# An attention stage's list scheduler with another model of transfers, and six load buffers instead of nine

## The chip, the cores and the metric

The kernel runs on one core of one Trainium2 chip. The metric is the device time of one execution, in microseconds. The kernel before takes 1522.84 us (median of 3 runs, 1522.7 to 1524.69).

## The reference

Three layers in float32, each fed by the one before. Attention has 8 batches, 8 heads, 576 query rows and head size 64; K and V are averaged over groups of 8 rows first, so that each query row sees 72 keys. Its output is read as 4608 tokens of 512 numbers for a mixture of 8 experts, in which each expert takes 576 tokens by a greedy choice over all logits; a gated layer follows.

```python
k_p = k.reshape(B, H, Sp, 8, D).mean(axis=3)
v_p = v.reshape(B, H, Sp, 8, D).mean(axis=3)
scores = np.matmul(q, k_p.transpose(0, 1, 3, 2)) / np.sqrt(D)
attn = np.exp(scores - scores.max(-1, keepdims=True))
attn = attn / (attn.sum(-1, keepdims=True) + 1e-9)
x = np.matmul(attn, v_p)                  # -> tokens, (4608, 512)
logits = x @ w_gate                       # expert e of each token, capacity 576
out[mask_e] = np.maximum(x[mask_e] @ w1[e], 0) @ w2[e]
y = (1 / (1 + np.exp(-(x2 @ wg))) * (x2 @ wv)) @ wo
```

## The kernel before

The program has three parts, one after another: `attention`, `experts` with the `Router` (which chooses the tokens), and `Gated`. The change touches `attention` and its scheduler alone.

Attention works on 18 tiles of 256 query rows: two for each batch (rows 0 to 511) and, after batches 3 and 7, one mixed tile with the last 64 rows of four batches. K and V come in 12 pieces each (`plan_kv`, L335): a load of 768 KB by SP's queue, three halvings that add pairs of rows (L341; VectorE for the first five K pieces, GpSimd for the others), a transpose on TensorE (L351) and a copy by ScalarE into kpT or vT (L357). From vT and the gate's weights (padded) TensorE makes the values of a batch, already multiplied by the gate (`plan_wv`, L382), which ScalarE copies into one of two buffers `wv` (L369). Three transfers inside the chip, the shift (L390 to L392, issued by ScalarE for batches 0 to 2 and by SP for the others), lay the same values out a second time at other partitions; a fourth (L394) copies them into `vmix` for the mixed tile. A buffer of wv may be written again, two batches later, when its tiles are done and its shift and vmix copy have landed.

For each tile, q is loaded by SP (L318; L323 with four small transfers for a mixed tile; two buffers of two tiles each), transposed (L411) and copied (L369). Chunks of two or three heads then go through scores (L448, `sps`), row maximum and subtraction on VectorE (L464, L468), exponential on ScalarE (L471), transposes (L484) and copies (L492), the product with the values (L509, L504, L518, `aps`), and VectorE's scaling by the row sums into `xt` (L526 to L533) and of the logits (L539, L542). SP stores the finished xt into `x_rows` (L551, L555). xt has three buffers, so a tile's first write waits for the store three tiles earlier.

The order of all engines' work is set by `Plan`, a list scheduler that runs while the program is built. Each operation has a cost on one or more engines; at each step `run` collects the operations that could start (`best`), takes those that start within 0.25 of the earliest, and emits the one of lowest rank (`go`). `go` also sets when the results are there. In the kernel before, a transfer of `size` > 0 runs on one path at 350 KB per us after those before it, and one of `size` < 0 (shift, vmix copy, stores of xt) ends a fixed time after its issue and takes nothing from the path:

```python
if x.size > 0:
    self.dma = max(self.dma, x.end + 1.3) + x.size / 350e3
    x.end = self.dma + 0.7
elif x.size < 0:
    x.end += 2.5 - x.size / 100e3
```

The plan's numbers only set the order; on the chip every engine waits for semaphores. Each transfer of SP and ScalarE takes the next of eight semaphores in rotation, and its issue waits until the transfer that held it has landed, with everything behind it in the same queue. The number of buffers of each tile stands in `BUFS`; `kv=9` are the loaded pieces of K and V.

Behind attention come the router's keys (`key_steps`; parts of it are scheduled in VectorE's gaps, L844 to L875), the first search over them, and then the experts.

Of the kernel before, what the change touches and what calls it, by code (L numbers as in the profile page):

```python
# [69 lines left out]
class Flow:  # L70
# [11 lines left out]
    def op(self, lanes, f, after=(), reads=(), makes=None, rank=0):  # L82
        x = Op(lanes, f, [a for a in after if a is not None], list(reads), makes, rank)
        if "tensor" not in lanes:
            self.todo.append(x)
        return x
# [68 lines left out]
class Plan(Flow):  # L155


    def __init__(self, nc):
        super().__init__(nc)
        self.dma = 0.0  # L160
        self.between = lambda gap: None
        self.held = {"vector": deque(maxlen=16), "gpsimd": deque(maxlen=16)}

    def op(self, lanes, f, after=(), reads=(), makes=None, rank=0, size=0, alone=False):
        x = Op(lanes, f, [a for a in after if a is not None], list(reads), makes, rank)
        x.size, x.alone = size, alone
        for b in x.reads:
            b.left = (b.left or 0) + 1
        self.todo.append(x)
        return x  # L170
# [16 lines left out]
    def best(self, x):  # L187
        at = self.ready(x)
        if at is None:
            return None  # L190
        lane = min(x.lanes, key=lambda n: max(self.t[n], at) + x.lanes[n])
        start = max(self.t[lane], at)
        if x.alone:
            for a, z in self.held["gpsimd" if lane == "vector" else "vector"]:
                if a <= start < z:
                    start = z
        return start, lane
# [13 lines left out]
    def go(self, x, lane, start):  # L211
        if lane == "tensor":
            self.between(start - self.t[lane])
        if x.makes is not None and x.makes.ap is None:
            self.free[x.makes.tag].popleft()
        x.f(getattr(self.nc, lane))
        x.lane, x.start = lane, start
        x.end = self.t[lane] = start + x.lanes[lane]
        if x.alone:
            self.held[lane].append((start, x.end))  # L220
        if x.size > 0:
            self.dma = max(self.dma, x.end + 1.3) + x.size / 350e3
            x.end = self.dma + 0.7
        elif x.size < 0:
            x.end += 2.5 - x.size / 100e3
        for b in x.reads:
            b.left -= 1
            b.end = max(b.end, x.end)
            if b.left == 0:
                self.free[b.tag].append(b.end)  # L230
        self.todo.remove(x)


def attention(tc, c, q, k, v, w_gate, xD, L, router, scr):
    nc = tc.nc
    ident = c["ident"]
    with ExitStack() as ctx:
# [21 lines left out]

        fl = Plan(nc)  # L260
        fl.t["gpsimd"], fl.t["vector"], fl.t["sync"] = 6.0, 3.0, 1.0
        BUFS = dict(kv=9, q2=2, qps=4, sps=1, aps=2, mx=3, sd=3, e=7, eT=4, qT=5, rs=3, xt=3)
        for tag, n in BUFS.items():
            fl.give(tag, n)
        count = {"av": 0}
# [26 lines left out]
        of_mix = {n: [y for y, (ti, _, _) in enumerate(chunks) if tiles[ti][1] is None and tiles[ti][0] == n] for n in range(2)}  # L292
# [8 lines left out]
        R = {}  # L301
# [9 lines left out]
        def load_q(ti, halves, rank):  # L311
            n, b, jj = tiles[ti]
            t = Buf("q2", None)
            for h0, h1 in halves:
                def f(eng, h0=h0, h1=h1):
                    qt = tile_of(t, loads, [128, H, 4, D])
                    if b is not None:
                        eng.dma_start(qt[:, h0:h1].rearrange("p h r d -> p h (r d)"),  # L318
                                      dram(q, b * H * S * D + h0 * S * D, [[4 * D, 128], [S * D, h1 - h0], [1, 4 * D]]))
                        return  # L320
                    for s in range(2):
                        for r in range(2):
                            eng.dma_start(qt[64 * s:64 * s + 64, :, r, :],  # L323
                                          dram(q, (4 * n + 2 * s + r) * H * S * D + 512 * D, [[D, 64], [S * D, H], [1, D]]))
                R["lq", ti, h0] = fl.op({"sync": 0.6 if b is not None else 2.4}, f, makes=t, rank=rank, size=(h1 - h0) * 131072)
            return t

        def plan_kv(ch, name, rank):
# [44 lines left out]
        def plan_wv(b, rank):  # L373
            free = [R["av", y] for y in of_b.get(b - 2, [])] + ([R["shift", b - 2], R["shiftm", b - 2]] if b > 1 else [R["wv1"]] * b)
            done = []
# [12 lines left out]
            def shift(eng):  # L388
# [1 line left out]
                eng.dma_start(w[72:108, 1], w[0:36, 0])  # L390
                eng.dma_start(w[0:36, 2], w[36:72, 0])
                eng.dma_start(w[36:108, 3], w[0:72, 0])  # L392
            R["shift", b] = fl.op({"scalar": 2.4} if b < 3 else {"sync": 2.2}, shift, after=done + free, rank=rank, size=-350000 if b < 3 else -165000)
            R["shiftm", b] = fl.op({"sync": 0.6}, lambda eng: eng.dma_start(vmix[:, b % 4], wv[b % 2][0:72, 0]),  # L394
                                   after=done + [R["av", y] for y in (of_mix[0] if b > 3 else [])], rank=rank + 5, size=-165000)

        def plan_q(ti):
            n, b, jj = tiles[ti]
# [55 lines left out]
        def plan_chunk(y, out):  # L454
            ti, h0, nh = chunks[y]
# [92 lines left out]
            def store(eng):  # L548
# [4 lines left out]
                for s in range(2):  # L553
                    for r in range(2):
                        eng.dma_start(dram(xD, ((4 * n + 2 * s + r) * S + 512) * DM, [[DM, 64], [1, DM]]),  # L555
                                      xt[64 * s:64 * s + 64, r].rearrange("p h d -> p (h d)"))
            fl.op({"sync": 0.6 if b is not None else 2.4}, store, after=[n2], reads=[out], rank=y, size=-524288)

        def loads_of(b):
            r = fb[b] - 12  # L560
# [1269 lines left out]
```

## Time and profile before

| | |
|---|---|
| median of 3 runs | 1522.84 us (1522.7 to 1524.69) |
| the profiled execution | 1523.92 us, span 1522.3 us |
| TensorE busy | 1467.1 us, 96% |
| weight loads busy | 1314.7 us, 86% |
| VectorE busy | 1059.7 us, 70% |
| ScalarE busy | 538.3 us, 35% |
| GpSimd busy | 395.7 us, 26% |
| moved by DMA | 294.22 MB, mean 193 GB/s |

Busy time is a sum over the whole span. Attention is the first 175 us or so, and there the engines are much less even than the sums say. In the section below, PE is TensorE, PEld its weight loads, DVE VectorE, ACT ScalarE, POOL GpSimd and SP the engine that issues most transfers; SPq is its queue. A wait is named by who waited and by what came last. Names like `kv` are the program's buffers, with their numbers left out.

### The profile page before, as it was taken

Reading aid. Unit: us, or ns where it says so; the run is one execution under the profiler, and the core shown is the slowest. Engines: PE = TensorE matmul, PEld = TensorE weight load, DVE = VectorE, ACT = ScalarE, POOL = GpSimd, SP = SyncE. Lnnn points to the kernel's source line nnn. Section 1 sums busy time; section 2 is a strip of 40 time slices with the busy share of each in tenths; the row PEclk is TensorE's granted clock in tenths of the full one; section 3 lists DMA queues with packets and bytes.
Section 4 is the critical chain, followed back from the end, with each engine's and each line's share of the span. In section 5 each row is a group of like instructions: output and inputs, shape, how many; then the busy total and the mean of one; then the engine's idle time right before and its main releaser. Section 6 shows DMA issues by size and latency. Waiting matters only on the chain.

```text
span 1522.3 us, 27187 instructions
## 1 busy us (share of the span) xinstructions
PE 1467.1 (96%) x10625; PEld 1314.7 (86%) x10625; DVE 1059.7 (70%) x2344; ACT 538.3 (35%) x1063; POOL 395.7 (26%) x416
## 2 busy tenths in 40 slices
PE   7889799999999999998999999999999999999997
PEld 5789669999999999997788888888888889999996
DVE  6688788889889977327778845666555764674564
ACT  4566232443434444334434322222321322232221
POOL 6870041353334422244323220012100120011001
PEclk9999789999999999999999999999999999999999
DMA  9974245356545686137655574535445365656651
GB/s 336 304 250 161 98 143 205 95 179 225 190 130 176 206 262 197 62 128 280 239 218 205 186 267 141 221 139 202 185 173 200 111 257 214 235 191 239 249 193 43
DMA packets 109330, 294.22 MB, mean 193 GB/s; under 512 B 12589, under 2 KB 43345, under 8 KB 94993
## 3 DMA queue, kind: packets, MB, share of 16 engines
q1 hardware_dynamic: 101636, 270.48, 50.0%
q0 software_dynamic: 6496, 20.98, 4.1%
q8 instruction: 84, 1.38, 0.4%
q10 hardware_dynamic: 1068, 1.03, 0.3%
q14 instruction: 46, 0.37, 0.1%
HBM read 222.33 MB, written 66.08 MB: 189 GB/s over the span
## 4 chain that ended last, share of the span: by engine, by line
PE 81%; DVE 8%; DMA 5%; issue 2%; ACT 1%; POOL 1%; SPq 0%; POOLq 0%; DVEq 0%; ACTq 0%
PE pj L1667 18%; PE hps L607 12%; PE acc L607 12%; PE Yg L1569 7%; PE Yv L1569 7%; PE Xg L1569 5%; PE Xv L1569 4%; PE Zg L1569 4%; PE Zv L1569 4%; PE rps L607 2%; PE aps L509 2%; DVE cx L607 1%; PE qps L484 1%; PE sps L448 1%; DMA q<-in_q_dram 1%
## 5 line engine op out<-in xcount | busy, mean ns | idle before, releaser
L607 PE MATMUL acc<-hh,w 128*128 128x288 f32 x1024 | 245.7, 304 | 0.0
L607 PE MATMUL hps<-xh,w 128*128 128x288 f32 x1024 | 235.3, 300 | 1.8 <-DVE hl L607 1.7
L1681 DVE TENSOR_TENSOR stg<-pj,stg 128x512 f32<-128x512 f32 x180 | 123.8, 689 | 109.0 <-PE pj L1667 108.1
L607 PEld LDWEIGHTS hps<-xh,w 128*128 128x128 f32 x1024 | 174.7, 189 | 3.0 <-DVE hl L607 2.4
L607 PEld LDWEIGHTS acc<-hh,w 128*128 128x128 f32 x1024 | 176.7, 189 | 0.2
L607 PE MATMUL acc<-hl,w 128*128 128x288 f32 x512 | 151.5, 296 | 0.9 <-DVE hl L607 0.9
L607 PE MATMUL hps<-xl,w 128*128 128x288 f32 x512 | 151.5, 296 | 0.1
L607 POOL TENSOR_TENSOR w<-stg,w 128x512 fp32r<-128x512 f32 (+1 forms) x81 | 119.5, 1489 | 116.2 <-ACT w L607 110.1
L607 ACT ACTIVATE hh<-hps 128x288 fp32r<-128x288 f32 x128 | 52.6, 411 | 252.4 <-PE hps L607 237.2
L1569 PE MATMUL Yg<-w 128*128 128x512 f32 (+1 forms) x540 | 126.9, 370 | 3.8 <-ACT w L1467 3.8
L1569 PE MATMUL Yv<-w 128*128 128x512 f32 (+1 forms) x540 | 126.2, 369 | 0.0
L1569 PEld LDWEIGHTS Yg<-w 128*128 128x128 f32 x540 | 99.9, 189 | 20.0 <-ACT w L1467 4.1
L607 POOL DMA_INDIRECT xg<-x_rows,idxs x48 | 46.4, 968 | 250.3 <-DVE capv L607 93.2
L1569 PEld LDWEIGHTS Yv<-w 128*128 128x128 f32 x540 | 99.4, 189 | 13.1 <-DVE vc L1605 0.4
L1667 PE MATMUL pj<-woh,xg 128*128 128x512 f32 x396 | 98.8, 391 | 1.5 <-DVE woh L1536 0.7
L1667 PE MATMUL pj<-woh,cw 128*128 128x512 f32 x396 | 98.7, 390 | 0.0
L607 PEld LDWEIGHTS acc<-hl,w 128*128 128x128 f32 x512 | 97.0, 189 | 1.1 <-DVE hl L607 1.1
L607 PEld LDWEIGHTS hps<-xl,w 128*128 128x128 f32 x512 | 96.8, 189 | 0.3 <-DVE xl L607 0.3
L1635 ACT ACTIVATE sg<-sg 128x512 f32<-128x512 f32 (+1 forms) x90 | 53.0, 589 | 122.6 <-DVE sg L1606 73.4
L607 DVE SCALAR_TENSOR_TENSOR hl<-hps,hh 128x288 fp32r<-128x288 f32 x128 | 57.4, 452 | 54.6 <-ACT hh L607 53.4
L607 ACT ACTIVATE w<-stg 128x512 fp32r<-128x512 f32 (+1 forms) x138 | 81.0, 638 | 35.8 <-DMA stg<-in_moe_w_dram 30.5
L1667 PEld LDWEIGHTS pj<-woh,xg 128*128 128x128 f32 x396 | 73.9, 188 | 17.3 <-DVE woh L1536 1.1
(280 smaller groups left out, 2968.4 us busy)
## 6 DMA issues: line engine op xcount, KB each, us to landing
w<-w_split SPq DMA_DIRECT2D x84, 1024.0 KB
stg<-in_moe_w_dram SPq DMA_DIRECT2D x30, 1024.0 KB
w_split<-w SPq DMA_DIRECT2D x21, 1024.0 KB
woh<-wo_split SPq DMA_DIRECT2D x24, 512.0 KB
wr<-wo_split SPq DMA_DIRECT2D x12, 1024.0 KB
kv<-in_k_dram SPq DMA_DIRECT2D x12, 768.0 KB
kv<-in_v_dram SPq DMA_DIRECT2D x12, 768.0 KB
x_cols<-x SPq DMA_DIRECT2D x16, 576.0 KB
```

The costliest lines, as they stand in the source:

```text
L448: eng.matmul(p[cs, r, G * j:G * j + G], t.ap[rs, h % 4, cs], kpT[rs, b if b is not None else 4 * n + 2 * c + r, h], start=True, stop=True)
L484: eng.transpose(p[:z, j], flat[:, a:a + z], ident)
L509: eng.matmul(p[:, a + s:a + s + 2], t[:, j + s], flat[:, x0:x1 + 1:x1 - x0], start=a + s == 0, stop=True, skip_group_check=True)
L607: r = f(*args, **kw)
L1569: eng.matmul(t, W(a, k), X(b, k), start=first and n == 0, stop=n == 5, skip_group_check=True)
L1635: x = fl.op(A, lambda eng: eng.activation(T(g), T(g), AF.Sigmoid), after=[op], rank=rank)
L1667: eng.matmul(self.tile(ps), G(a), W(b), start=n == 0, stop=n == 5)
L1681: y = fl.op({"vector": 0.69}, lambda eng: eng.tensor_tensor(A(), self.tile(ps), A(), op=OP.add), after=[x, st["acc", u, i]], reads=[ps], r ...
```

## The change

`Plan` now keeps the landing times of all transfers (`flights`). A transfer can start no earlier than the eighth before it has landed. A transfer from SP runs on the one path whatever its kind, at a rate of its own: 350 KB per us, and 110 for shifts and vmix copies. An operation that issues several transfers counts as so many (`dmas`), each with its share. ScalarE's shifts take places among the eight, not the path. `kv` has six buffers.

```diff
+        self.flights = [0.0] * 8
...
-    def op(self, lanes, f, after=(), reads=(), makes=None, rank=0, size=0, alone=False):
+    def op(self, lanes, f, after=(), reads=(), makes=None, rank=0, size=0, alone=False, rate=350e3, dmas=1):
         x = Op(lanes, f, [a for a in after if a is not None], list(reads), makes, rank)
-        x.size, x.alone = size, alone
+        x.size, x.alone, x.rate, x.dmas = size, alone, rate, dmas
...
         start = max(self.t[lane], at)
+        if x.size:
+            start = max(start, self.flights[-8] + 0.1)
...
-        if x.size > 0:
-            self.dma = max(self.dma, x.end + 1.3) + x.size / 350e3
+        if x.size and lane == "sync":
+            for i in range(x.dmas):
+                x.end = max(x.end, self.flights[-8] + 0.4)
+                self.t[lane] = x.end
+                self.dma = max(self.dma, x.end + 1.3) + x.size / x.dmas / x.rate
+                self.flights.append(self.dma + 0.7)
             x.end = self.dma + 0.7
-        elif x.size < 0:
-            x.end += 2.5 - x.size / 100e3
+        elif x.size:
+            x.end += 2.5 + 2 * x.size / x.rate
+            self.flights += [x.end] * x.dmas
...
-        BUFS = dict(kv=9, q2=2, qps=4, sps=1, aps=2, mx=3, sd=3, e=7, eT=4, qT=5, rs=3, xt=3)
+        BUFS = dict(kv=6, q2=2, qps=4, sps=1, aps=2, mx=3, sd=3, e=7, eT=4, qT=5, rs=3, xt=3)
...
-                R["lq", ti, h0] = fl.op({"sync": 0.6 if b is not None else 2.4}, f, makes=t, rank=rank, size=(h1 - h0) * 131072)
+                R["lq", ti, h0] = fl.op({"sync": 0.6 if b is not None else 2.4}, f, makes=t, rank=rank, size=(h1 - h0) * 131072, dmas=1 if b is not None else 4)
...
-            R["shift", b] = fl.op({"scalar": 2.4} if b < 3 else {"sync": 2.2}, shift, after=done + free, rank=rank, size=-350000 if b < 3 else -165000)
+            R["shift", b] = fl.op({"scalar": 2.4} if b < 3 else {"sync": 2.2}, shift, after=done + free, rank=rank, size=336384, rate=110e3, dmas=3)
             R["shiftm", b] = fl.op({"sync": 0.6}, lambda eng: eng.dma_start(vmix[:, b % 4], wv[b % 2][0:72, 0]),
-                                   after=done + [R["av", y] for y in (of_mix[0] if b > 3 else [])], rank=rank + 5, size=-165000)
+                                   after=done + [R["av", y] for y in (of_mix[0] if b > 3 else [])], rank=rank + 5, size=168192, rate=110e3)
...
-            fl.op({"sync": 0.6 if b is not None else 2.4}, store, after=[n2], reads=[out], rank=y, size=-524288)
+            fl.op({"sync": 0.6 if b is not None else 2.4}, store, after=[n2], reads=[out], rank=y, size=524288, dmas=1 if b is not None else 4)
```

The lines of the changed kernel stand eight further down from `go` on (L318 is L326 there, L394 is L402, L551 is L559). No instruction of attention is added or removed; they change places, up to the last of attention, and the order behind it is the same on every engine.

SP's queue, from the eighth load of K and V on (first before, then now). `q_232` and `q_255` are q of batch 2; the vmix copy from `wv_124` is batch 0's.

```order
L335 DMA kv<-in_k_dram 128x3x512 x2
L335 DMA kv<-in_v_dram 128x3x512 x2
L335 DMA kv<-in_k_dram 128x3x512
L318 DMA q_232<-in_q_dram 128x4x256 x2
L335 DMA kv<-in_v_dram 128x3x512
L335 DMA kv<-in_k_dram 128x3x512 x2
L394 DMA vmix<-wv_124 72x584
```

```order
L343 DMA kv<-in_k_dram 128x3x512 x2
L326 DMA q_255<-in_q_dram 128x4x256 x2
L343 DMA kv<-in_v_dram 128x3x512 x2
L343 DMA kv<-in_k_dram 128x3x512
L402 DMA vmix<-wv_124 72x584
L559 DMA x_rows<-xt 128x1024
```

The vmix copy moved ahead of one V and two K loads, and q of batch 2 ahead of two V loads and a K load.

SP's queue around the first mixed tile's q (`q_816` before, `q_774` now), before and now:

```order
L551 DMA x_rows<-xt 128x1024
L394 DMA vmix<-wv_124 72x584
L335 DMA kv<-in_k_dram 128x3x512
L335 DMA kv<-in_v_dram 128x3x512
L323 DMA q_816<-in_q_dram 64x8x64 x4
L551 DMA x_rows<-xt 128x1024 x2
```

```order
L326 DMA q_594<-in_q_dram 128x4x256 x2
L343 DMA kv<-in_v_dram 128x3x512
L559 DMA x_rows<-xt 128x1024
L331 DMA q_774<-in_q_dram 64x8x64 x4
L402 DMA vmix<-wv_124 72x584
L559 DMA x_rows<-xt 128x1024
L343 DMA kv<-in_k_dram 128x3x512 x2
L343 DMA kv<-in_v_dram 128x3x512
L559 DMA x_rows<-xt 128x1024
```

The K and V loads that stood ahead of the four transfers now stand behind them and behind the next store.

VectorE at the end of attention, before and now; `L<-lm` is the last reduction of the logits, and kh, u, C, EoU and kl belong to the router's keys.

```order
L533 TENSOR_TENSOR xt<-aps,rs 128x2x128
L539 TENSOR_TENSOR lm<-aps,rs 128x2x16
L542 TENSOR_REDUCE L<-lm 128x16
L864 TENSOR_TENSOR T_105<-M,U 128x10
L866 CAST kh<-V 128x10
L868 TENSOR_SCALAR u<-u 128x10
L870 TENSOR_TENSOR C<-kh,tr_77 128x10x15
L873 SCALAR_TENSOR_TENSOR EoU<-P,T_105 128x80
L875 CAST kl<-u 128x10
```

```order
L878 TENSOR_TENSOR C<-kh,tr_77 128x10x15
L881 SCALAR_TENSOR_TENSOR EoU<-P,T_105 128x80
L883 CAST kl<-u 128x10
L534 TENSOR_SCALAR rs<-aps 128x4
L535 RECIPROCAL rs<-rs 128x4
L541 TENSOR_TENSOR xt<-aps,rs 128x2x128
L547 TENSOR_TENSOR lm<-aps,rs 128x2x16
L550 TENSOR_REDUCE L<-lm 128x16
```

The six operations on these columns moved ahead of the last tile's scaling.

## Rows read from the trace of the kernel before

**Rows 1.** The page's head: the span of the profiled execution.

```profile
span 1522.3 us, 27187 instructions
```

**Rows 2.** Busy time by stretch; columns in its first line (PEclk: granted share of 2.4 GHz).

```profile
core 0: us, PE busy (x) PEld busy (x) DVE busy (x) ACT busy (x) POOL busy (x), PEclk, DMA share, GB/s
...
44.00:50.00 6.00, 0.69 (x4) 0.70 (x4) 0.86 (x2) 1.15 (x3) 5.69 (x7) 0.69 0.98 303
50.00:54.00 4.00, 4.00 (x21) 3.91 (x20) 0.89 (x4) 1.54 (x5) 3.11 (x3) 0.61 1.02 364
54.00:76.00 22.00, 21.65 (x367) 20.39 (x365) 16.91 (x55) 14.50 (x34) 19.96 (x18) 1.00 1.06 289
76.00:82.00 6.00, 3.22 (x35) 2.56 (x38) 3.40 (x9) 3.35 (x9) 5.29 (x26) 0.87 0.87 297
82.00:88.00 6.00, 6.00 (x61) 5.86 (x55) 3.64 (x12) 3.31 (x8) 5.08 (x19) 0.56 0.97 346
...
100.00:152.00 52.00, 50.03 (x817) 45.73 (x816) 45.13 (x153) 33.85 (x78) 9.47 (x12) 1.00 0.49 154
```

**Rows 3.** Waits of TensorE in the attention stage, 0 to 176 us.

```profile
PE qps L351 <- DVE kv L341: 6.4, 2, 3.8
PE qps L411 <- ACT wv L369: 5.6, 1, 5.6
PE sps L448 <- DVE sd L468: 2.5, 2, 1.4
...
PE aps L509 <- DVE lm L539: 1.3, 1, 1.3
```

**Rows 4.** Waits of all engines, 0 to 260 us: two that ended with a transfer.

```profile
ACT wv L369 <- DMA vmix<-wv: 6.6, 1, 6.6
...
DVE xt L533 <- DMA x_rows<-xt: 5.9, 2, 5.0
```

**Rows 5.** Timeline of SP's queue: start us, us until the last was issued, what.

```profile
16.58 4.14 SPq L335 DMA_DIRECT2D kv<-in_v_dram  x2
...
25.87 2.35 SPq L318 DMA_DIRECT2D q<-in_q_dram  x2
...
33.99 2.44 SPq L335 DMA_DIRECT2D kv<-in_k_dram  x2
37.55 0.95 SPq L394 DMA_DIRECT2D vmix<-wv  x1
...
58.20 0.34 SPq L551 DMA_DIRECT2D x_rows<-xt  x1
...
62.21 8.36 SPq L323 DMA_DIRECT2D q<-in_q_dram  x4
70.68 3.77 SPq L551 DMA_DIRECT2D x_rows<-xt  x2
```

**Rows 6.** Timeline of all engines, 0 to 60 us: a transpose that frees a buffer.

```profile
20.95 0.55 PE L351 MATMUL qps<-identf,kv 128*128 128x128 f32 x3
```

**Rows 7.** Timeline of all engines, 38 to 70 us: the first stall's end.

```profile
48.85 0.41 ACT L369 ACTIVATE wv<-qps 72x288 f32<-72x288 f32 x1 [6.65 <-DMA vmix<-wv]
...
49.31 1.11 PE L411 MATMUL qps<-identf,q 128*128 128x128 f32 x4 [5.57 <-ACT wv L369]
```

**Rows 8.** Timeline of all engines, 70 to 105 us: the second stall's end.

```profile
78.32 0.56 DVE L533 TENSOR_TENSOR xt<-aps,rs 128x384 f32<-128x384 f32 x1 [5.04 <-DMA x_rows<-xt]
```

**Rows 9.** Groups of instructions by shape, 0 to 178 us: GpSimd's three halvings.

```profile
L341 POOL TENSOR_TENSOR kv<-kv 128x768 f32<-128x768 f32 x19 | 34.6, 1823 | 15.5 <-DMA kv<-in_v_dram 15.4
...
L341 POOL TENSOR_TENSOR kv<-kv 128x384 f32<-128x384 f32 x19 | 19.7, 1038 | 1.3
...
L341 POOL TENSOR_TENSOR kv<-kv 128x192 f32<-128x192 f32 x19 | 11.3, 592 | 1.5
```

**Rows 10.** Timeline of VectorE: router's key work after the last reduction of the logits.

```profile
174.96 0.16 DVE L864 TENSOR_TENSOR T<-M,U 128x10 f32<-128x10 f32 x1
...
175.62 0.17 DVE L875 CAST kl<-u 128x10 f32<-128x10 int32 x1
```

## The prediction

> **What bounds the kernel now.** I looked at the span first, then at busy time by stretch, then at TensorE's waits in the stage that the change touches, and last at SP's queue in that stage, because the change only reorders attention. The profiled execution took 1523.92 us, 1522.3 of them span [rows 1], so 1.6 lie around it. It stands 1.1 us above the median of the three runs shown (1522.84) and inside their range.
>
> In most of the program TensorE is the bound, and after attention every engine's order is the same in both kernels. So an attention stage that ends earlier moves the rest forward by as much, and only its waits matter. In [rows 2] the reader is to see how uneven the stage is: from 100 to 152 us TensorE is busy 50.03 of 52 us at full clock; from 44 to 50 us it does 0.69 of 6; from 76 to 82 us 3.22 of 6. After both holes the granted clock is low: 0.61 of full from 50 to 54 us and 0.56 from 82 to 88 us, where 0.5 is the lower level of 1.2 GHz. What the engine did before each fall is nearly nothing for five microseconds in the first, two waits close together in the second. The DMA share is 0.98 in the first hole and 0.87 in the second, with hardly less around them, while from 100 to 152 us it is 0.49: everything is loaded early, and small urgent transfers share the path with loads that nobody needs yet.
>
> TensorE's own waits [rows 3] name four: 6.4 us for halved rows (3.8 at the start, so 2.6 later), 5.6 for ScalarE's copy into wv, 1.4 at most for sd, 1.3 for lm. Behind two of these stands a transfer [rows 4]: ScalarE waited 6.6 us for the vmix copy, VectorE 5.0 us for a store of xt.
>
> **First hole: the vmix copy.** Batch 2's rows may enter wv only when batch 0's copy from wv to vmix has landed. SP issued that copy at 37.55 us, after the two K loads of 33.99 us [rows 5]; ScalarE went on at 48.85 and TensorE at 49.31, after 5.57 us of nothing [rows 7]. From the issue's end (38.50) to the release are 10.3 us, which the copy spent behind other loads. The first pair of lists shows the change: two K loads and one V load fewer stand ahead of it. At the 303 GB/s of the first hole [rows 2] these 2.36 MB are 7.8 us, 2.2 more than the hole is long. q of batch 2 moves ahead of two V loads; its two parts (1.05 MB, 3.5 us at that rate) delay V. That V was issued from 16.58 us on [rows 5] and feeds the copies into wv that wait in the hole, more than 20 us later; halving a piece takes GpSimd 1.82 + 1.04 + 0.59 = 3.45 us [rows 9]. Between load and use there is room for both, so I cost the delay at nothing; if this cover is gone it is at most 3.5 us. I take the hole as removed: 5.6 us. The clock comes with it: 4.00 us of work at 0.61 lost 4.00 x 0.39 = 1.6 us, and the 0.69 us before it at half clock lost 0.3. **First term: 5.6 + 1.9 = 7.5 us.**
>
> **Second hole: the store of xt.** xt has three buffers, so a tile's first write waits for the store of the tile three before. The store of 70.68 us stood behind four transfers of the mixed tile's q, which took SP from 62.21 to 70.57 because each waited for a place among eight [rows 5], and those places were held by K and V loads. VectorE then stood 5.04 us [rows 8], TensorE 1.3 and 1.4 [rows 3], and 6.00 us at 0.56 lost 6.00 x 0.44 = 2.6. The second pair of lists: the four still come before a store, but the K and V loads that stood right ahead of them now follow that store, and the places that the four need were last held by parts of q, a vmix copy and a store. **Second term: 1.3 + 1.4 + 2.6 = 5.3 us.**
>
> **Tail.** Six operations of the router's keys ran after the last reduction of the logits, from 174.96 to the last one's start at 175.62 [rows 10]; now they stand ahead of it (third pair), in slots where VectorE waits for the last tiles. **Third term: 0.7 us.**
>
> **Six buffers instead of nine.** A load now waits for the transpose six loads earlier. The fifth and sixth waits of this kind decide: V of batch 2's second piece waits for a transpose that ended at 21.50 us [rows 6], where SP issued it at 20.72 [rows 5]. That is 0.8 us later, with other loads in flight and the DMA share near 1, so it costs nothing on the path; if it did, 0.8 us. The wait for halved rows of 2.6 us stays: the same K pieces are loaded and halved in the same order.
>
> **The remaining moves** are TensorE's and VectorE's order over 18 tiles. K and V of batches 4 to 7 are now halved, transposed and copied between those tiles' work and not before it. No row shows the cost. Below, nothing or a gain: the holes already counted hold all the waits of more than 2.6 us that are named. Above, one more wait like the first hole with its clock, 7.5 us. Nearer than either is how full TensorE is in an undisturbed stretch: 0.35 us idle in 22 where loads are plenty, 1.97 in 52 later [rows 2]. If the 50 us after the first hole run like the latter, that is 1.9 - 0.8 = 1.1 us more; a shift of wv (three issues, then a landing that no row isolates) that comes a little late twice would add about 2. I take 3 us.
>
> **Sum.** 7.5 + 5.3 + 0.7 - 3 = 10.5 us. From 1523.9 that is 1513.4; from the median it would be 1512.3. I forecast 1513.
>
> **A rule that speaks against it.** In the first hole the buffers are full and TensorE still waits, so depth is not what it lacks. The Trainium skill (Perfetto Trace Analysis, "Optimization Strategy") says that gaps that recur on the engine that should be saturated can mean too few buffers for the next tile. By that rule three buffers fewer would open gaps; the trace agrees with it nowhere in this stage, since no wait of TensorE ends with a K or V buffer coming free. The third rival works out what it would do.
>
> **The rivals.**
> *Only one hole closes.* The vmix copy also needs one of eight places, and the one it takes is held by a shift that ScalarE issues into the same crowded path; if that lands late, the copy still lands after 44 us. Then the second term and the tail remain: 5.3 + 0.7 - 3 = 3 us, 1521; or the first alone: 7.5 + 0.7 - 3 = 5.2, 1519. For it: landing took 10 us in this queue. Against it: three loads fewer. Chance 0.17, about half of it within 0.2% of before.
> *The model does not match the chip.* The planner's new rates (350 GB/s, 110 GB/s for copies inside the chip) set an order that the chip runs otherwise, and the waits come at other places for the same sum: 1520 to 1526. For it: 256-byte pieces of the mixed tile's q, which one rate cannot describe; the DMA moved 289 GB/s there with its share at 1.06 [rows 2]. Against it: the urgent copies really come earlier in SP's list. Chance 0.10.
> *Loads come too late (slower).* With six buffers and the loads of batches 4 to 7 behind stores that wait for VectorE, a piece reaches the path: 0.79 MB at 303 GB/s is 2.6 us, halving 3.45, together 6.0, and each such hole lowers the clock as above, 1.9 more. One or two eat part or all of the gain; from three (23.7 us against 13.5) the kernel is slower, 1534. For it: the stores from 70.68 us held the queue for 3.77 us [rows 5]. Against it: those loads stand tens of rows of SP's list ahead of their use, and the path is half idle after 100 us. Chance 0.08.
>
> **How the numbers follow.** 0.2% is 3.0 us, about what a measurement of this kernel tells from no change. The forecast has 0.65 (1507 to 1518: all terms and no new wait give 1523.9 - 13.5 = 1510.4 against the profiled run, 1509.3 against the median, and 2.6 more if the wait for halved rows goes too; on the other side 7.5 for new waits gives 1517.9). Faster by over 3.0 us: 0.65 + 0.08 = 0.73 and 0.02 of the second rival, 0.75. Within: 0.09 + 0.06 = 0.15. Slower: 0.02 + 0.08 = 0.10. For 8 in 10 the range goes from 1507 up to 1521, into the first rival.
>
> **What would show it.** Right: no wait of ScalarE for vmix and none of VectorE for x_rows above 1 us; the granted clock full from 30 us to the last tile; the last reduction of the logits near 164 us instead of 174.7; the six key operations before it; the router's phase and all after it as long as before. Wrong in the first step: ScalarE's copy into wv still waits for vmix between 40 and 50 us. Wrong in the costs at nothing: TensorE's transposes of kv wait for GpSimd, or aps for a shift of wv, after 50 us. The forecast falls if attention ends within 3 us of where it ended.

## The result and the profile of the changed kernel

The changed kernel takes **1507.12 us** (median of 4 runs, 1506.83 to 1510.05), the kernel before 1522.77 beside it (4 runs, 1522.06 to 1524.69): ratio 0.9900, 95% interval 0.9882 to 0.9917. That is 15.65 us less, where the forecast was 1513 in a range from 1507 to 1521: the sign was right, the gain too small by a third, and the time lies just above the lower end of that range. The profiled execution took 1506.83 us, its span 1505.2.

The same view as [rows 2], of the changed kernel:

```profile
core 0: us, PE busy (x) PEld busy (x) DVE busy (x) ACT busy (x) POOL busy (x), PEclk, DMA share, GB/s
...
44.00:50.00 6.00, 5.69 (x90) 5.15 (x87) 4.00 (x13) 2.30 (x6) 1.39 (x3) 1.00 1.11 299
50.00:54.00 4.00, 3.06 (x24) 2.82 (x24) 2.87 (x11) 2.45 (x7) 3.07 (x3) 1.00 0.91 230
54.00:76.00 22.00, 21.27 (x354) 19.68 (x353) 18.88 (x60) 14.78 (x33) 14.73 (x14) 1.00 1.02 334
76.00:82.00 6.00, 6.00 (x101) 5.77 (x95) 5.51 (x18) 3.64 (x9) 5.65 (x15) 1.00 1.05 392
82.00:88.00 6.00, 6.00 (x78) 5.46 (x77) 5.39 (x22) 5.09 (x14) 5.66 (x12) 1.00 1.05 372
...
100.00:152.00 52.00, 48.72 (x764) 45.03 (x765) 46.77 (x155) 30.94 (x72) 20.38 (x47) 1.00 0.51 167
```

From 44 to 50 us TensorE is now busy 5.69 us of 6 where it was 0.69, from 76 to 82 us 6.00 where it was 3.22, and the granted clock is 1.00 in every one of these stretches. From 50 to 54 us it idles for 0.94 us of 4, which it did not before, and from 100 to 152 us it does less (48.72 us of 52 against 50.03). Its waits up to 176 us, as in [rows 3]:

```profile
PE qps L359 <- DVE kv L349: 3.8, 1, 3.8
...
PE qps L359 <- POOL kv L349: 1.9, 3, 0.9
...
PE sps L456 <- DVE sd L476: 1.5, 3, 0.8
...
PE aps L517 <- ACT eT L500: 1.4, 2, 0.9
```

The wait for ScalarE's copy into wv (5.6 us) is gone, and so is the second wait for rows halved by VectorE: 6.4 us in two became 3.8 in one, the one at the start. In its place stand three short waits for GpSimd's halving, 1.9 us together. No wait of ScalarE for vmix and none of VectorE for x_rows is left in attention, which answers [rows 4]. SP's queue, as in [rows 5]:

```profile
31.52 0.94 SPq L402 DMA_DIRECT2D vmix<-wv  x1
...
36.95 3.59 SPq L326 DMA_DIRECT2D q<-in_q_dram  x2
...
42.67 4.59 SPq L331 DMA_DIRECT2D q<-in_q_dram  x4
...
51.59 0.45 SPq L559 DMA_DIRECT2D x_rows<-xt  x1
```

The vmix copy is issued at 31.52 us instead of 37.55. The four transfers of the mixed tile's q are issued from 42.67 us on and take SP 4.59 us; they were issued from 62.21 on and took 8.36. The end of the stage, as in [rows 10], and the first step of the router's search behind it (178.34 us in the trace of the kernel before):

```profile
160.70 0.38 DVE L550 TENSOR_REDUCE L<-lm 128x16 f32<-128x128 f32 x1
161.12 0.20 DVE L852 TENSOR_SCALAR L<-L 128x80 f32<-128x80 f32 x1
...
163.78 0.15 DVE L615 TENSOR_SCALAR_CACHE_REDUCE hit<-acc 15x8 f32<-15x8 f32 x1 [0.50 <-PE acc L615]
```

To see where the time came from, take from VectorE's timeline the start of the last reduction of the logits of each tile, in the order in which they come, and subtract it from that of the kernel before. These **leads** are the column heads of the next table. For the changed kernel: 3.0 us at the second tile, 7.2 at the third, 7.1 at the fifth, 13.6 at the seventh, 12.1 at the seventeenth, 14.0 at the last, 14.6 at the search. So 3.0 us came before the first hole, 4.2 in it, 6.5 in the second (from the fifth tile to the seventh), and only about 1 in all the rest. A lead is read from one profile of each kernel and can be off by 2 or 3 us: in experiment 5 below nothing is changed that acts before the third tile, and its leads at the second and third are -2.8 and 1.7 us. The span shrank by 17.1 us, 2.5 more than attention did. What follows attention has the same order in both, and in the profiles of this study it took from 1340 to 1348 us whatever the kernel, so these 2.5 us aren't attributed.

### The profile page after: what moved, and what is told of

Its sections match the earlier page's. It is cut to its first block, busy times and chain, and to the rows that moved or that the text cites. A ratio compares the mean times of both kernels' runs of the same rounds, so it can differ in the third digit from the quotient of the medians.

```text
span 1505.2 us, 27177 instructions
## 1 busy us (share of the span) xinstructions
PE 1459.1 (97%) x10625; PEld 1309.6 (87%) x10625; DVE 1059.7 (70%) x2344; ACT 537.8 (36%) x1063; POOL 395.5 (26%) x416
## 4 chain that ended last, share of the span: by engine, by line
PE 82%; DVE 9%; DMA 4%; issue 2%; POOL 1%; SPq 1%; ACT 0%; POOLq 0%; ACTq 0%; DVEq 0%
PE pj L1675 19%; PE hps L615 12%; PE acc L615 12%; PE Yv L1577 7%; PE Yg L1577 7%; PE Zg L1577 5%; PE Xg L1577 5%; PE Xv L1577 5%; PE Zv L1577 5%; DMA kv<-in_v_dram 2%; PE rps L615 2%; PE aps L517 2%; DVE cx L615 1%; PE qps L492 1%; PE sps L456 1%
## 5 line engine op out<-in xcount | busy, mean ns | idle before, releaser
L1577 PEld LDWEIGHTS Yv<-w 128*128 128x128 f32 x540 | 99.5, 189 | 13.6 <-DVE vc L1613 0.8
L1675 PEld LDWEIGHTS pj<-woh,xg 128*128 128x128 f32 x396 | 74.0, 188 | 15.8 <-DVE woh L1544 1.1
```

The costliest lines, as they stand in the source:

```text
L1577: eng.matmul(t, W(a, k), X(b, k), start=first and n == 0, stop=n == 5, skip_group_check=True)
L1675: eng.matmul(self.tile(ps), G(a), W(b), start=n == 0, stop=n == 5)
```

## The experiments

Each group of kernels ran on a chip of its own with the kernel before beside it. The ratio is to that kernel, and only ratios and leads (us against the trace of the kernel before) are compared between groups.

| kernel | median, before beside it | ratio, 95% interval | lead at tile 3 | tile 5 | tile 7 | search |
|---|---|---|---|---|---|---|
| changed | 1507.12, 1522.77 | 0.9882 to 0.9917 | 7.2 | 7.1 | 13.6 | 14.6 |
| 1 old model, six | 1513.00, 1522.73 | 0.9914 to 0.9947 | 4.3 | 7.1 | 7.4 | 8.4 |
| 2 new model, nine | 1512.05, 1522.73 | 0.9909 to 0.9943 | 9.3 | 7.7 | 12.3 | 11.7 |
| 3 path only, six | 1510.93, 1522.73 | 0.9905 to 0.9938 | 7.3 | 8.1 | 11.6 | 10.7 |
| 4 eight only, six | 1517.89, 1522.73 | 0.9951 to 0.9979 | 3.5 | 5.3 | 12.6 | 3.7 |
| 5 fourth xt | 1515.65, 1522.37 | 0.9941 to 0.9975 | 1.7 | 2.5 | 6.2 | 5.3 |
| 6 third wv | 1519.25, 1522.37 | 0.9974 to 1.0000 | 4.6 | 0.9 | 3.3 | 3.6 |
| 7 both buffers | 1517.48, 1522.37 | 0.9957 to 0.9978 | 7.5 | 8.3 | 5.2 | 6.3 |
| 8 GpSimd beside | 1507.89, 1522.37 | 0.9891 to 0.9924 | 5.5 | 5.7 | 12.6 | 12.3 |
| 9 tokens later | 1511.83, 1525.83 | 0.9898 to 0.9925 | 7.1 | 6.7 | 13.6 | 12.9 |
| 10 path, tokens later | 1514.02, 1525.83 | 0.9905 to 0.9936 | 6.2 | 7.2 | 10.8 | 11.3 |
| 11 both, q earlier | 1526.03, 1525.83 | 0.9995 to 1.0015 | 4.3 | 5.2 | -4.3 | -2.5 |
| 12 same order, nine | 1510.83, 1525.28 | 0.9890 to 0.9928 | 7.5 | 7.9 | 14.8 | 16.7 |

### One part of the change at a time

**1.** The kernel before with one number changed.

```diff
-        BUFS = dict(kv=9, q2=2, qps=4, sps=1, aps=2, mx=3, sd=3, e=7, eT=4, qT=5, rs=3, xt=3)
+        BUFS = dict(kv=6, q2=2, qps=4, sps=1, aps=2, mx=3, sd=3, e=7, eT=4, qT=5, rs=3, xt=3)
```

> The kernel before with six load buffers instead of nine and nothing else (the old model of transfers). Its list of SP already has q of batch 2 ahead of two V loads and the vmix copy of batch 0 one load earlier still; but the four transfers of the first mixed tile's q stay behind a store, two loads and a vmix copy, and two stores follow them. Theory A (the model of transfers sets the better order, the buffers are a detail): the first hole closes, the second stays: 1513 to 1517 us, a DVE wait for x_rows of over 2 us between 60 and 85 us. Theory B (six buffers alone do it, since loads that nobody needs yet cannot be issued): 1506 to 1510, no DVE wait for x_rows over 1 us.

1513.0, as theory A has it: the first hole closes, the second stays. VectorE's waits (us in total, times, longest):

```profile
DVE xt L533 <- DMA x_rows<-xt: 6.0, 1, 6.0
```

Busy time by stretch, with the columns of [rows 2], shows TensorE's idle time and the clock behind it:

```profile
72.00:76.00 4.00, 1.36 (x34) 1.25 (x38) 3.35 (x9) 1.52 (x3) 2.58 (x3) 1.00 0.98 344
76.00:82.00 6.00, 6.00 (x92) 5.71 (x85) 4.96 (x18) 3.15 (x7) 2.55 (x2) 0.72 1.02 367
```

The four transfers of the mixed tile's q took 5.45 us of SP here. The 9.7 us come from the buffers alone, through the order that the planner makes of them: it cannot place loads that have no buffer, so q of batch 2 and the vmix copy come first.

**2.** The changed kernel with `kv=9`.

> The changed kernel with nine load buffers instead of six (the new model alone). The vmix copy of batch 0 stands where the changed kernel has it; five K and V loads stand between two stores ahead of the mixed tile's q. Theory A (the model sets the order): 1506 to 1511 us, both holes closed. Theory B (the six buffers do it): 1515 to 1523, with one of the two holes open again, by the five loads in a row the second one.

1512.05, just above A's range. Both holes are closed (lead 12.3 at the seventh tile), no wait of VectorE for x_rows is left, and the four transfers of the mixed tile's q take 4.41 us. So either part of the change closes the first hole, and of the two only the model closes the second. What is missing to the changed kernel appears in the traces over the last tiles: at the thirteenth the leads are 14.0 and 14.1 us, at the search 11.7 and 14.6. The two intervals just overlap, and what in the order of the last tiles makes this difference stays open.

**3 and 4.** Each half of the model alone, with six buffers. In 3 the two lines that read `flights` are taken out; in 4 a transfer without a new tile (stores, shifts, vmix copies) is taken off the path:

```diff
-                self.dma = max(self.dma, x.end + 1.3) + x.size / x.dmas / x.rate
-                self.flights.append(self.dma + 0.7)
+                if x.makes is not None:
+                    self.dma = max(self.dma, x.end + 1.3) + x.size / x.dmas / x.rate
+                    self.flights.append(self.dma + 0.7)
+                else:
+                    self.flights.append(x.end + 2.5 + x.size / x.dmas / 100e3)
-            x.end = self.dma + 0.7
+            x.end = self.flights[-1]
```

> The changed kernel with the limit of eight in flight taken out of the planner: all transfers of SP still share one path at their rates, six buffers. If the limit of eight is what places the mixed tile's four transfers rightly (theory A1): they are issued while places are held by K and V loads, VectorE waits for a store of xt by over 2 us, the second hole is back, 1512 to 1516 us. If the one path is what matters (theory A2): 1506 to 1510.

> The changed kernel with the limit of eight in flight kept in the planner, but stores, shifts and vmix copies of SP taken off the one path (they land a fixed time after their issue, as in the kernel before); six buffers. Theory A1 (the limit of eight places the mixed tile's transfers): 1506 to 1511 us, no DVE wait for x_rows over 1 us. Theory A2 (the one path is what matters): 1512 to 1520, with one of the two holes open.

1510.93 and 1517.89: theory A1 falls on both counts. A2 has the time of 4 right, but not the reason: neither ScalarE's wait for vmix nor VectorE's for x_rows is back in it. With the path alone the second hole is closed (VectorE's one wait for x_rows is 0.5 us, the four transfers take 3.65 us of SP). With the limit of eight alone they stand at almost the time of the changed kernel, 42.74 us, but one more K load is in flight, and they hold SP's queue more than twice as long. From SP's timeline (start, us until the last was issued):

```profile
42.74 9.85 SPq L334 DMA_DIRECT2D q<-in_q_dram  x4
```

K and V behind them come late, as TensorE's waits show:

```profile
PE qps L362 <- POOL kv L352: 4.5, 3, 2.2
```

That is the mechanism of the prediction's slower rival, loads that come too late, but it explains only a part. The lead falls from 12.6 us at the seventh tile to 9.5 at the eighth, where the longest of these waits (2.2 us) ends and the granted clock is 0.72 of full from 82 to 88 us. It falls by another 5.8 us up to the search, with no such wait after 90 us; VectorE is busy for 5.5 to 5.7 us of every 6 from 100 to 118 us there. What took these 5.8 us stays open.

### The two holes by themselves

**5, 6, 7.** These keep the order of the kernel before on every engine and take away only what was waited for, by a buffer more in memory than the planner counts (7: both). The fourth buffer is xt's alone, though the expectation names lm too; in 7 lm has two, which VectorE alone writes and reads. The last two lines of the second cut stand for each place that uses wv, and GpSimd clears the third buffer with the second.

```diff
-                    out.ap = work.tile([128, 2, H, D], F32, name="xt", bufs=3), work.tile([128, 2, H, E], F32, name="lm", bufs=3)
+                    out.ap = work.tile([128, 2, H, D], F32, name="xt", bufs=4), work.tile([128, 2, H, E], F32, name="lm", bufs=3)
```

```diff
-        wv = [const.tile([108, 4, H, 73], F32, name=f"wv{i}") for i in range(2)]
+        wv = [const.tile([108, 4, H, 73], F32, name=f"wv{i}") for i in range(3)]
...
-wv[b % 2]
+wv[b % 3]
```

> The kernel before with a fourth buffer of xt and lm and nothing else; the planner still counts three, so every engine's order is that of the kernel before. Only the wait for the store of three tiles earlier goes. Theory D (the second hole is the late store of xt): VectorE's wait of 5.0 us for x_rows goes, the granted clock is full from 82 to 88 us, 1515.5 to 1518 us (5.3 us less by the prediction's second term, 6.5 by what the changed kernel gained between its sixth and seventh tile). Rival: VectorE then waits for something else that is as late (scores, q of the mixed tile): 1520 to 1523.

> The kernel before with a third buffer of wv (cleared by GpSimd with the second, while it is idle before 13 us) and nothing else; the planner still counts two, so the order is that of the kernel before. Batch 2's rows need not wait for batch 0's copy to vmix. Theory E (the first hole is the late vmix copy): no ACT wait for vmix, clock full from 50 to 54 us, and 1515 us by the prediction's first term (7.5 us), or 1518.5 if it is worth only the 4.3 us that the changed kernel gained from its second to its third tile. Rival: halved V or q of batch 2 or 3 is late too, and less than 3 us comes: 1520 to 1523.

> The kernel before with the third wv and the fourth xt together (lm with two buffers, which VectorE alone uses), in the order of the kernel before. If the two holes are independent and what the changed order gives is the end of these two waits: 1510 us by the prediction's two terms (12.8 us), 1512 by 4.3 and 6.5. If the crowded path makes other things late once the two waits are gone: 1515 to 1519.

By medians the gains are 6.7, 3.1 and 4.9 us. The interval of 6 reaches no change and those of 5 and 7 overlap, so which of the three is fastest is not settled. What is clear is that both together give far less than the 12.8 or 10.8 us of two independent holes.

5 bears theory D out: its time lies in the range, no wait of VectorE for x_rows is left, and the granted clock stays full where it fell to 0.56:

```profile
76.00:82.00 6.00, 5.19 (x77) 5.07 (x78) 3.46 (x11) 3.64 (x8) 5.16 (x25) 1.00 0.85 287
82.00:88.00 6.00, 6.00 (x125) 5.54 (x124) 5.52 (x19) 4.00 (x10) 5.15 (x18) 1.00 0.98 349
```

The first hole is worth what was predicted, **at its place**: in 7 the lead goes from 0.2 us at the second tile to 7.5 at the third, in 6 from -2.8 to 4.6, 7.3 us each. But not all of it lasts. In 6 the second tile came 2.8 us late, in an order that is that of the kernel before (see the last section), and the lead falls from 4.6 us at the third tile to 3.3 at the seventh. VectorE waits 9.2 us for stores where it waited 5.9 [rows 4]:

```profile
DVE xt L533 <- DMA x_rows<-xt: 9.2, 2, 4.7
```

In 7 VectorE waits only 1.2 us for a store, but TensorE waits for q of the mixed tile:

```profile
PE qps L411 <- DMA q<-in_q_dram: 5.8, 1, 5.8
```

Busy time by stretch around it:

```profile
72.00:76.00 4.00, 0.87 (x4) 0.90 (x5) 0.00 (x0) 0.00 (x0) 3.84 (x4) 0.76 1.02 316
76.00:82.00 6.00, 6.00 (x67) 5.72 (x66) 3.29 (x9) 1.74 (x4) 5.30 (x26) 0.59 0.92 271
```

TensorE does 0.87 us of work in 4, the clock falls to 0.59, and the lead drops from 8.3 at the fifth tile to 4.8 at the sixth. So once TensorE comes to the second hole earlier, the late store is one of two late things in it: q of the mixed tile, ahead of the store in SP's queue, is late itself. In 5, which came to the fifth tile 5.8 us later than 7, no wait of TensorE for this q is seen.

**11.** As 7, with the mixed tile's q planned earlier by hand:

```diff
-                R["q", 8 + n] = load_q(9 * n + 8, ((0, 8),), first[9 * n + 8] - 14)
+                R["q", 8 + n] = load_q(9 * n + 8, ((0, 8),), first[9 * n + 8] - 18)
```

> The kernel before with a third wv, a fourth xt (as in the seventh experiment) and the rank of the mixed tile's q lowered by four, which puts its four transfers right behind the first vmix copy and ahead of q of batch 3; old model, nine buffers. If what held the seventh experiment at a gain of 5 us was the place of the mixed tile's q in SP's queue: no PE wait for q of over 2 us, attention ends 4 to 6 us earlier than there, 1511 to 1513 us. Rival (these four transfers hold SP's queue wherever they stand, and then batch 3's q or V comes late, as in the fourth experiment): another wait of 3 to 6 us between 50 and 90 us, 1516 to 1520.

The rival holds, and more than that: 1526.03, no gain at all. Issued from 39.09 us on, behind two K loads and a vmix copy, the four transfers hold SP's queue for 11.7 us, by SP's timeline:

```profile
39.09 11.69 SPq L323 DMA_DIRECT2D q<-in_q_dram  x4
```

q of the next batches then comes late, by TensorE's waits:

```profile
PE qps L411 <- DMA q<-in_q_dram: 8.4, 2, 6.0
```

So with both buffers the second hole stays (7), and the earlier place opens another (11). The lower rank moves other work as well, so 11 does not isolate the place.

What closes the second hole in the changed kernel is not isolated either. The time for which the four transfers hold SP's queue goes with it, but not sharply. In the changed kernel, 8, 9 and 12 it is 2.98 to 5.11 us, in 2, 3 and 10 it is 4.41, 3.65 and 6.27, and no hole follows in any of them. In the order of the kernel before (with 5, 6 and 7) it is 8.36 to 9.78, in 1, 4 and 11 it is 5.45, 9.85 and 11.69. But one hole followed at 5.45 (1), none at 6.27 (10), and in 5, at 9.78, TensorE loses only 1.6 us between 72 and 82. SP's timeline of 10:

```profile
53.65 6.27 SPq L330 DMA_DIRECT2D q<-in_q_dram  x4
```

### VectorE's halving and GpSimd

VectorE's halvings of the fourth and fifth K piece are the same instructions in both kernels. In groups by shape, from 24 to 37 us (count, us busy, mean ns of one), the kernel before:

```profile
L341 DVE TENSOR_TENSOR kv<-kv 128x384 f32<-128x384 f32 x2 | 2.6, 1299 | 0.0
L341 DVE TENSOR_TENSOR kv<-kv 128x768 f32<-128x768 f32 x2 | 2.2, 1100 | 0.0
L341 DVE TENSOR_TENSOR kv<-kv 128x192 f32<-128x192 f32 x2 | 1.4, 694 | 0.1
```

And the changed kernel:

```profile
L349 DVE TENSOR_TENSOR kv<-kv 128x768 f32<-128x768 f32 x2 | 1.9, 950 | 0.0
...
L349 DVE TENSOR_TENSOR kv<-kv 128x384 f32<-128x384 f32 x2 | 1.1, 551 | 0.0
...
L349 DVE TENSOR_TENSOR kv<-kv 128x192 f32<-128x192 f32 x2 | 0.7, 358 | 0.1
```

Together 6.2 us against 3.7, and 2.2 of the 2.5 us are the two shorter shapes. In the kernel before GpSimd halves V from 30.51 us on; now, with q of batch 2 ahead of that V, it starts at 35.00. The other profiles go with it: in 5, 6, 7 and 11, in the old order, 128x384 takes 1298 to 1302 ns and 128x192 694 to 696; in 1, 2, 3, 4, 9, 10 and 12, where GpSimd starts that V from 34.58 us on or later, 547 to 558 and 357 to 359. 128x768 varies from 948 to 1114 ns over all of these and does not follow. **8** puts GpSimd's reading back, for nothing:

```diff
+            def first_halving(eng):
+                if name == "k" and ch in (3, 4):
+                    waste = work.tile([128, 3, 4, D], F32, name="waste", bufs=1)
+                    nc.gpsimd.tensor_tensor(waste, raw.ap[:, :, 4:8], raw.ap[:, :, 4:8], op=OP.add)
+                halve(4)(eng)
-            a0 = fl.op(wide(768, early), halve(4), after=[ld], rank=rank, alone=True)
+            a0 = fl.op(wide(768, early), first_halving, after=[ld], rank=rank, alone=True)
```

> The changed kernel with two more additions on GpSimd, 128x768 into a buffer that nobody reads, one for each of the fourth and fifth K piece, which start when that piece has landed, as VectorE's first halving of it does. GpSimd is idle there (28 to 35 us) and all other orders are the same. Theory C (VectorE's halving is held up while GpSimd reads the same memory): the halvings of these pieces take 4 to 5 us instead of 2.8, the second tile's logits come 1.5 to 2.5 us later than 40.4 us, and some of it stays in the time: 1507.5 to 1510 us. Rival (VectorE was slow in the kernel before for another reason): the halvings stay at 2.8 us, 1506.5 to 1507.5.

The same groups in this kernel:

```profile
L349 DVE TENSOR_TENSOR kv<-kv 128x768 f32<-128x768 f32 x2 | 2.9, 1450 | 0.0
L349 DVE TENSOR_TENSOR kv<-kv 128x384 f32<-128x384 f32 x2 | 2.4, 1205 | 0.0
...
L349 DVE TENSOR_TENSOR kv<-kv 128x192 f32<-128x192 f32 x2 | 0.7, 358 | 0.1
```

The two shapes that meet GpSimd's additions (1.47 us each) go from 950 to 1450 and from 551 to 1205 ns; the third, after them, keeps its 358. The second tile comes 2.6 us later than in the changed kernel (43.02 against 40.39). Theory C is shown for these instructions. The Trainium skill (SBUF — State Buffer, "Who interferes with whom") says that a VectorE instruction with both inputs in SBUF contends with a GpSimd instruction that reads SBUF, and that one of the two stands until the other has finished; the trace agrees, with 551 ns alone and 1299 beside GpSimd (128x384). How much of the 2.6 us reaches the end isn't settled: the profiled execution, the slowest of four (1512.91; the others 1507.32 to 1508.24), has 2.3 us less lead at the search, but by the ratios, 0.9908 against 0.9900, it is about 1 us, inside the intervals.

**9 and 10** try the same cause at another place. Five token steps of the router run on VectorE, but the planner counts them as GpSimd's and so does not keep them apart from GpSimd's halving:

```diff
...
+            R["t", i] = fl.op({"vector": 0.2}, lambda eng: next(toks, None), after=[R.get(("t", i - 1)), R["c", 87], R["L", 12]], rank=40)
...
```

> The changed kernel, in which the five steps of the router's token tables that run on VectorE (casts and integer operations of 128x36), planned before as GpSimd steps, are planned on VectorE after the thirteenth tile, when GpSimd has halved its last piece. Theory C (VectorE's operations on two buffers, and its casts, stand while GpSimd reads): the two slow ones of 1.03 and 0.64 us take 0.17 to 0.18 each, TensorE loses about 1 us less between 118 and 128 us, attention ends 1 to 2 us earlier, 1505 to 1506.5 us. Rival (VectorE was not the bound there): the same 1507.

> The planner with the one path alone and six buffers (as in the third experiment), and the five token steps on VectorE planned after the thirteenth tile. Theory C: the hole from 106 to 118 us, in which these five took 4.6 us instead of 0.9 while GpSimd halved and the clock fell to 0.55, goes: 5 to 6 us less than the 1510.9 of the third experiment, 1505 to 1506.5 us, as fast as the changed kernel. Rival (the hole came from late scores or late loads of batch 4): 1509 to 1512.

One of the five steps on VectorE's timeline of experiment 3, while GpSimd halves:

```profile
111.53 1.78 DVE L830 TENSOR_SCALAR tokt<-toki 128x36 int32<-128x36 int32 x1
```

The same step in 10, when GpSimd is done:

```profile
129.75 0.17 DVE L837 TENSOR_SCALAR tokt<-toki 128x36 int32<-128x36 int32 x1
```

Busy time by stretch in 3:

```profile
106.00:112.00 6.00, 2.98 (x76) 2.52 (x69) 5.76 (x16) 2.53 (x6) 5.68 (x7) 0.88 0.51 192
112.00:118.00 6.00, 6.00 (x58) 5.86 (x54) 5.17 (x11) 2.75 (x6) 2.86 (x3) 0.55 0.23 90
...
136.00:152.00 16.00, 15.63 (x258) 14.47 (x260) 14.61 (x47) 10.21 (x24) 0.00 (x0) 1.00 0.28 99
```

And in 10:

```profile
106.00:112.00 6.00, 4.65 (x111) 3.96 (x110) 5.55 (x19) 2.97 (x7) 5.69 (x7) 1.00 0.75 242
112.00:118.00 6.00, 6.00 (x89) 5.66 (x87) 4.08 (x11) 3.70 (x9) 2.82 (x3) 1.00 0.22 88
...
136.00:152.00 16.00, 14.66 (x260) 12.76 (x258) 14.41 (x47) 8.09 (x19) 0.00 (x0) 1.00 0.26 104
```

1.78 us against 0.17, and the hole shrinks: TensorE does 4.65 us instead of 2.98 from 106 to 112 us, and the clock no longer falls to 0.55. In 9 TensorE gains 1.6 us between 118 and 136 us in the same way. So theory C is right about the steps and wrong about their worth, since neither kernel is faster: 10 gains 11.8 us like 3, and 9 gains 14.0 against the changed kernel's 15.65, with intervals that overlap. The lead shows it: 3.1 us more than 3 at the eleventh tile in 10, 0.6 more at the search. From 136 to 152 us VectorE is busy 14.4 to 14.6 us of 16 in all of these, and TensorE less in 10, which got there earlier (15.63 us in 3, 14.66 in 10). That VectorE's load is the limit of the last tiles is the likeliest reading; no run tested it.

### The buffers by themselves

**12.** The changed kernel's order with nine buffers in memory:

```diff
-                b.ap = pool.tile(shape, F32, name=b.tag, bufs=BUFS[b.tag])
+                b.ap = pool.tile(shape, F32, name=b.tag, bufs=9 if b.tag == "kv" else BUFS[b.tag])
```

> The changed kernel with nine load buffers in memory while the planner still counts six: every engine's order is that of the changed kernel, only the waits of loads for a free buffer go. If six buffers cost nothing on the chip (the prediction's step for them) and the 5 us between the changed kernel and the second experiment (nine buffers in both) are a matter of order alone: the same gain as the changed kernel, 15 to 16 us below the kernel before on the same chip (ratio 0.99), attention's last reduction 160 to 161.5 us. If loads that wait for a buffer are what keeps the path free for urgent transfers (theory B), loads now start earlier and crowd it: 2 us or more of the gain goes, with ACT waiting for vmix or DVE for x_rows again. If waiting loads cost something, 1 to 3 us more gain.

Ratio 0.9909, 14.45 us: the changed kernel's gain within the intervals. Theory B, that a load's wait for a buffer keeps the path free, falls: no wait of ScalarE for vmix and none of VectorE for x_rows appears. Within what can be measured, six buffers work through the planner's order alone. The lead grows from 0.3 us more than the changed kernel's at the third tile to 2.2 more at the search, so waiting loads may cost a little; the times can't tell it. No version tried is faster than the changed kernel by more than its interval.

## Why the prediction came out as it did

**First term (7.5 us, the vmix copy).** Right in mechanism: ScalarE no longer waits for vmix. In size it holds in the order of the kernel before, 7.3 us across the hole in 6 and 7. In the changed kernel the lead grows by only 4.2 us there, from 3.0 to 7.2; TensorE's waits for GpSimd's halving (0.9 and 0.3 us) and for eT (0.9) between 40 and 52 us take a part of the rest. By itself the end of this wait is worth 3.1 us by the medians of 6, with an interval that reaches no change.

**Second term (5.3 us, the store of xt).** The size was near, 6.5 us between the fifth and the seventh tile. The reason was half of it: the prediction saw that the four transfers held the queue, but priced only the store behind them. 5 shows that the store is what VectorE waited for, 7 that behind a closed first hole the mixed tile's q is late as well (5.8 us), and 11 that putting it earlier by hand gave no gain.

**Third term (0.7 us, the key operations).** The lead grows by 0.6 us from the last reduction to the search.

**Six buffers (nothing).** Confirmed by 12 within what can be measured. The rule weighed against this step, that recurring gaps can mean too few buffers (the Trainium skill, Perfetto Trace Analysis, "Optimization Strategy"), is not borne out here: nine buffers in the same order change the time by nothing that can be measured, and six in the old model (1) make it 9.7 us shorter.

**"The wait for halved rows of 2.6 us stays."** This is the step that failed. It argued from VectorE's own order, which is the same, and did not ask what GpSimd does at that time. Moving q ahead of V, costed at nothing for the delay of V, took GpSimd's reading away from VectorE's halving and the wait with it: 3.0 us of lead at the second tile. Experiment 8 brings the long halvings back and 2.6 of these 3.0 us with them.

**New waits (-3 us).** The size was fair: the two terms as predicted and the halving make 7.5 + 5.3 + 3.0 = 15.8, and the lead at the seventh tile is 13.6, so 2.2 us went into new waits by then, as from 50 to 54 us. The stretch up to the seventeenth tile lost 1.5 more, and the tail gained 1.9 besides the third term. The sum of the prediction with the halving's 2.6 us added is 13.1 us; attention ended 14.6 us earlier, and the median fell by 15.65. That this is so near the lower end of the forecast's own case, 1509.3 - 2.6 = 1506.7 with no new wait, is in part luck: new waits did come, and 2.5 us of the shorter span lie behind attention, without a known cause.

**The rivals.** *Only one hole closes* is what six buffers with the old model give (1), at 1513.0 where the rival said 1519. *Loads come too late* is what the limit of eight without the path gives (4), in part, at 1517.9. The change met neither: with both rules in the model the second hole closes whatever the buffers (2), and TensorE's waits for GpSimd's halving come to 1.9 us in all.

## What to carry to other kernels

Price a stall twice: what it is worth at its place, and what is late next behind it. Two holes in one crowded queue need not be a sum, and taking one wait away by a buffer can give the time to the next wait; another order of the same transfers closed both. When a change moves work of one engine, look at what the neighbour that shares its memory does in the same microseconds, not only at that engine's own order.

## What was unexpected of the hardware

Four transfers of 64x8x64 elements held SP's queue for 2.98 us (8) to 11.69 (11), since each waits until the transfer that held its semaphore has landed.

VectorE's integer and cast steps of 128x36 elements take 0.17 us alone and up to 1.78 us while GpSimd halves, nearly as long as one of GpSimd's first halvings (1.82 us, [rows 9]); the maxima over scores in PSUM, between them, keep their 0.60 us.

The same gap does not always cost the clock. In the kernel before and in 5, whose order is the same, TensorE waited 2.6 us for VectorE's halving. The next transposes, from the kernel before and from 5:

```profile
34.23 0.52 PE L351 MATMUL qps<-identf,kv 128*128 128x128 f32 x3 [2.62 <-DVE kv L341]
```

```profile
34.00 0.87 PE L351 MATMUL qps<-identf,kv 128*128 128x128 f32 x3 [2.58 <-DVE kv L341]
```

In 5 the clock then went to the lower level of 1.2 GHz, in the kernel before not. Busy time by stretch in the kernel before:

```profile
34.00:36.00 2.00, 1.77 (x54) 1.55 (x55) 0.61 (x2) 0.97 (x2) 2.00 (x2) 1.00 1.08 354
```

And in 5:

```profile
34.00:36.00 2.00, 2.00 (x43) 1.67 (x47) 0.11 (x1) 0.96 (x2) 1.96 (x2) 0.50 1.08 352
```

6 did as 5. The second tile came 2.8 us later than in the kernel before in both, and 0.2 earlier in 7, where the wait was 2.2 us and the clock stayed full. A single profile's lead of 2 or 3 us at that place can be this and not the kernel.
